# A two-stage 3x3 convolution block on one core: six outer sums moved from adding transfers to VectorE, 13 more constant matmuls, another instruction order

## The chip, the core and the metric

The kernel runs on one core of a Trainium2 chip. The core has a matrix engine (TensorE, "PE" in the profile, with its weight loads "PEld"), VectorE ("DVE"), ScalarE ("ACT"), GpSimd ("POOL"), a queue engine that issues most transfers (SyncE, "SP"), and 16 DMA engines. Each engine works through its own queue in order and waits on semaphores for the others. The metric is device time of one execution in microseconds (us).

## The reference

```python
B, C, HW, E = 2, 512, 64, 1152
def gn(z, gamma, beta):            # group norm, 4 groups of 128 channels
    ...
def conv3(z, w):                   # 3x3, padding 1, as nine shifted einsums
    ...
h = conv3(_silu(gn(x, g1, be1)), w1)
h = h + (_silu(t_emb) @ w_emb).reshape(B, C, 1, 1)
h = conv3(_silu(gn(h, g2, be2)), w2)
return x + h
```

Two images of 512 channels, 64 x 64 points; two group norms with silu, each followed by a 3x3 convolution from 512 to 512 channels; a per-channel embedding is added between them and the input at the end. Inputs are bf16, the kernel computes in f16 with sums in f32.

## The kernel before

**Tiling.** Channels are cut into four tiles of 128 (the partitions): `ct` of the input, `k` of the output. Each image is cut into two halves of 32 rows, so there are eight chunks `c`: 0 and 1 the halves of image 0 in the first convolution, 2 and 3 those of image 1, 4 to 7 the same for the second. A unit is one chunk and one output tile (`unit(c, k)`, L818): 32 units.

**Fewer products.** The convolution over rows is done as a fast algorithm: VectorE forms six combinations ("planes" 0 to 5) of the rows of a chunk (`rows_a`, `rows_b`), VectorE and ScalarE form six combinations of the weights (`prep_w1`, `prep_w2`), TensorE multiplies plane by plane, and the results are added with small factors. Planes 0 to 3 are partly nested a second time over columns (`nest_w1`, `fetch_w2`, `vnest`). In a unit, ScalarE reads the finished sums from PSUM (`evac_o` for planes 4 and 5, `evac_m`, `evac_b`), and VectorE adds them up: S, A, s, d and y (L872 to L1015). The planes 4 and 5, the "outer" ones, must still be added to the first and last eight rows of the unit's result `ys`: the outer sum, 128 x 1040 elements. `CFG['oacc'][c]` says for how many of the four `k` this is done by an adding transfer that GpSimd issues (`dma(yo.ap, oo.ap, ..., sw=True, acc=True)`, named `oa`); for the others it is a `tensor_tensor` on VectorE (named `O`). In chunks 4 to 6 the result then goes to the output by another adding transfer from GpSimd's queue, onto the input that was copied there before (`pre`); in the first convolution it goes to `h_scr`. There are two buffers `ys`, used in turn.

**Opening.** The first image is loaded in eight pieces (`x0` and `x1`: first and second half of a channel tile), with the first weights between. `stats0` makes the group norm's sums: tile 0 by `bn_stats` on VectorE for the first half, by ScalarE (a square with its sum) and TensorE (products with ones) for the second; tiles 1 to 3 by TensorE (products with ones, and Gram products for the squares) for the first half, by ScalarE and TensorE for the second. `gn_chain` joins them with a few tiny f32 matmuls, VectorE and GpSimd instructions. Then `silu` (ScalarE) and `rows_a` and `rows_b` (VectorE) make the planes of chunk 0, and TensorE does planes 4 and 5 of units 0 to 2 first ("o"), since these need only `rows_a`. Before all that, TensorE multiplies constants: 11 matmuls `warm` and `CFG['fill']` matmuls `fill`, 128x128 by 128x512 ones into PSUM bank 5, which nothing reads (L1082 to L1085).

**Between.** `stats1` makes the sums of image 1 on ScalarE during chunk 0 (two passes of 2080 elements over each of eight pieces); `prod(c+1, k)` makes the planes of the next chunk while chunk `c` is multiplied; `prep_w2` makes the second convolution's weights and stores them in `u_scr`; `outer_kinds` and `outer_weights` make operands for chunk 7, whose planes 4 and 5 are nested too. The embedding's product is copied from PSUM by VectorE (L1105).

**Order.** Every operation is an `Op` of a plan with an engine and its dependencies. They are emitted in the order that the string `ORDER` gives (two characters for each operation, base 64), so the string fixes the order in every engine's queue. Matmuls of the units follow a chain that fixes their order among each other. All of it goes through a few helper lines, so the profile shows L348 for VectorE's tensor_tensor, L352 for its scalings, L371 for ScalarE, L386 for transfers and L401 for matmuls.

Of the kernel before, what the change touches and what calls it, by code (L numbers as in the profile page):

```python
# [115 lines left out]
def _idx(off, dims):  # L116
# [49 lines left out]


ORDER = (
    "0E09000B0A2T0C0G0F0D0c010H020304050607080b0I160a130R0Z140X0g0S0Y150d0f0e0T0h1817190i0j0U0k1A0l1B0K1C2M1D0m0n1u0L"
    "0o2J0V0W1E0v0M1N1X3C1F0O1G1Y0p1Z0y0J1r0r1a3K1b1_0q1H201Q0N1c2c221d0s211e1I0t1f23241g4g0_1h3E251J0u2U261i271j0w28"  # L170
    "1K291k3F0x100Q0z120-2A3D1L1l2B1M1m1O1n2C4L111P1o1R2f1S4T3H1p2D1q1x2F1s3L2E1t1y1v2G1w1T2e2P2H2i2I3G2K1U2Q1-2L0P2N"
    "2W2O1V2X1z2l2Y1W2m3g2V2Z2R2n2b4O2h2d2o2S2p3a2a2q3X4N2r3M2s3N3h2g4M2t3i3O2u3P2v4U2k2w2x3Q2j2y3R2_2z3S3Z3j3d2-3k3u"
    "303T5P323v3U4V313w4Q3J5H4X3x4W3y3I3V3z4P333-4Y3_343l374Z423c3m3543366L3W443Y4a453b465J4S4h4k4738485K5Q493e394q3r"
    "4b3n4r3o4e4B4s5I4c4t4R3f4u4m4v406D4n4A4w414x4f4j6Y4-5R4_4d6M505T3p6Z513q525L6a535U547u556F5V5S5c4l3s5X4i5d7v5e4C"
    "6E5f7w5h5W5i4D4G4o5jB74EB85k4p3A4F5l5M4H5m5n3t5Z4I5Y5o566G8y575r4z6N5s4y5a5tB9583B5u5b5w6P5x595C5N5y6O5A6Q5z5BBB"
    "5-5v6RBN8z5_5g7h6S6I605D616b4J6T5E6H6c6U6d8l8-6e6XBA6W6g5q6h6iBFBCBP6j6kBD5p6l6mA06n626sBO6VBG636t6JBE5O6KA14K6u"
    "A25F6vB46x646y6w6z6-65686_7071BRBH727666B5BJ6777D56f6978DDBQ7PBIBT796A6o7Q6pBS7A7RB6DE737BBU7S6r5G7TBL7CBK7D7UBM"
    "7V7W7x7X747Y7Z7y7aD67E7b6q7z7c7F7d75DG7-7eDF7f7G80D781827gDH7i8384D985Ee86DJ87DL8C7H8DDI7I7j8E7JD27K8F7l888H7k8G"
    "8I8J8K8m7m8L8M8ND39p8O7n8S7L8T897p8U6B7M7_7o8VDN8A8W8Q7q8a8XD4D88n8Y8PDB8Z8o8_8bDA8p909qDMDC7r918q928BAt947s6C95"
    "9697988r998R9ADK9B9G7t7O8c9HEf8s9IDP9J8tEm9L8d9M9N9O8w8f9P9Q9R8e9S8x9W8g8u9XEg8h939Y9C9ZDOEi8i9D9r9aEuEh9F7N9bAu"  # L180
    "DR9cDQ9s9d9tA39UEn8vA49K9u9TA59ECr9e9vA69V9fA89xA9A7AA8jAB9gACAD9wAE9kAFAK9hAGAHAL9y9jAMEkEoAvAN9iEjAPEpAQAxElCs"
    "ARAS9-ATAUAVAWAa9lEvAbDS9zAX9mAcAyAYAdAw8kAeAzEO9_AfAIA_AgAiA-AhAJBVAjB09nBWEwAZCtBXB3AkBYB2BaBbAoBcAlBdAOBeBfCv"
    "AnBgBhBlCuAmBmBnBjBoApBiBtBZBuBpCwAqBkBvEyBq9oBwEbGJB1ByBzCQEqB-B_CREcC0GBC1CxExC2CTEdC3BxC6CUCzC7C8C4C9EsCCCAEr"
    "CDC5CyEtAsCEE-CVC-CFFxEzDTBrGLDUC_GDGKE_CGDVCSBsEPCWD1DWGCD0DYDZDaDbCBDcDdDgDeDfGFEQDjCXCHDkDlCYG8DmDrGNDhCZCIDs"
    "HhGECaGRG9DtCKCbERGMDuCLCJCcESDwFyDxDyCdGADzD-CeETD_E0E1CME4HUE5E6DoE7DnEAGHDiCNCfEBDXEUArGPE2ECGGDvEVEDGSHjEWF0"
    "GTCgGOE3F1GIChE8EXF2DqFzF3CiDpGQF5CjEaF6F7GVF8F9EEE9FAHpFBFCFEFGHVHlFHFIFJEFHxFOEYHiFPCkF_GUFQEGFLFREZEIFTEJFUEH"
    "FVG0FWFFFXFYF4GWFZFaEKFDFdFeHrFfFgHkFjG1FKELClGXFkFbF-HqFSFlGYJ6FMFcFmHtFhCOG2GZCPCmHnGaCnHmGbG3GcHzFNHyI3FnG5Ge"
    "GfJ7GgHsG7GhGiG4GnGjGmGkGlFiHWGpJ8GqHoGrGsHuGxFoEMGyHvGuKNGoGzFpGtCpG-HYI4FrHwFsH0G6H1H2ENH3H4CoHZH5H6H7FqHAHaHB"
    "FtHCHDH-HGG_HXFuHHGdGwKPHII5KOHbHEHJCqHcI6IBH9GvHKICHdNMH8IDHgJ9HfIENLIGHFIHIIIJIKI7ILIMHLINIRIQISH_ITHPIUHMIZIP"
    "I0IOIaHOHNI9IbIWI1IVIcIFI8I2HeIeJAIfHQIgIhFvIiIjIkIlIXHRIoInIpJCIqIAIdIrIuIYImJDIvIsJBIwJEItKQIxJGJSJLJFJTJUJHIy"  # L190
    "JJJVKRJXJYJZIzJaJbJcI-FwJdMvJeLeJiKTJjLfJkJlJIJqKSJ0JrKUOzI_JsJ1JKJtLgJfMxO-J2KVJvJwJgJxJhJyMwKXJzJ-JWJ_KWK0JnK3"
    "K4JuJMK5K6JmKbK9K1KYKAK2KaK7KBLhKCKZKjKcJNKkJoKDKlJ3LiKmJpJOKoKpKqK8KrKsKnKtKuLkKvKxKzMyJPK-HSK_L0KEL5LlL6LjLmL7"
    "KFKIOiL8OjKwJQLAKHNHNGLBLoLCKGLDLELnQBLFKyLGJRLHHTLKLLOkLpNJLMLNLQLrLROxL1L2KJLSMzQALTLsL-L4L_L9M_LIM0M-LJM1N0Pv"
    "LUM3L3PwM4LOM5KdM6N1M7M8LPM9J5MAJ4MEMFKeMGMHLVMMLqNKMCMNMDLWMOLZKKLXMPN2MBKLMRLYMSKfMTMUM2MVN3MWMJMXPxLtMIMYLaMb"
    "KMMcMdMeMhN6MiMQMLMjMZN4MkMaMKNNMfN7NOMlOyKgOlNPMgN8NQOHN5NSNTMmNUNVOmNWLbNXNYNZOIKhNbMnNcMqOKOnNdMoOoR5RMMpNFNe"
    "KiLdNgNhMrQ8NiNjNkNlNmOpLcNnNRNrNsMsNtOqNuNvLuNaNwQ9NxNyOrMuN-OLLvN_O0O1OsO2O3O4LwO5O_NfOMOJLxNoP0ONOwP1NzNpP2Nq"
    "O6P4OtP5P6PyP7O7OOP8P9PAOPPBLyPDO8PzPELzPFRKO9PGN9OAR7PIR6P-PJOCPKPLNAOBPMPNP3POOvPPMtPTPCPUPVPWP_PXPQPYPZRLODPa"
    "PcPHPdPePfQ0PgOEPhPiSZPRPjQ1QCPSOFPkQDOuTlPbQESHNINBQFQ3R8QHPlSIQIOGQJQKQLQMQ2QNQOQQPmNCQRPqPnQSQ5PoQTQ4PpQVSXQW"
# [1192 lines left out]
```

## Time and profile before

| | us |
|---|---|
| three runs | 460.74, 462.39, 459.73 |
| median | 460.74 |
| the profiled execution | 462.31 |
| its span, first to last instruction | 460.5 |
| TensorE busy | 448.6 |
| VectorE busy | 436.9 |
| ScalarE busy | 402.8 |
| GpSimd busy | 57.8 |
| mean granted TensorE clock | 0.992 |

The page gives each engine's busy time over the span; the 40 slices show it over time, in tenths; the table of stages gives it in us for any stretch, with the granted clock, the share of the DMA engines and GB/s at the end of the line. The groups of instructions have a mean duration, in which neighbours overlap, so what one more instruction costs is read from start to start. The list of waits says who waited for whom. An operation's place in the order string is matched to the trace by counting each engine's instructions. Twenty-six adding transfers `ar<-ar` are in the profile, 22 of 260 KB and 4 of 130 KB (the outer sums of the first two units of chunk 4 are done in two pieces).

### The profile page before, as it was taken

The numbers are of one execution on the slowest core, as the hardware profiler recorded it, in microseconds if no ns is written. First come the engines' busy times: TensorE is split into PE (matmuls) and PEld (weight loads), VectorE is DVE, ScalarE is ACT, GpSimd is POOL, SyncE is SP. The second block draws the span as 40 slices with busy tenths as digits, with TensorE's granted clock in tenths as the row PEclk, the third lists the DMA queues.
The fourth block names the chain that finished last, engine by engine and source line by source line (L and its number), as shares of the span: only waits on it lengthen the run. The fifth ranks groups of instructions, "written<-read, shape, count | busy, mean of one in ns | idle before, by whom it ended". The sixth has DMA issues, their size and how long they took to land. (4 is left out here: it accounts for less than half of the span.)

```text
span 460.5 us, 8098 instructions
## 1 busy us (share of the span) xinstructions
PE 448.6 (97%) x2891; PEld 282.0 (61%) x2891; DVE 436.9 (95%) x811; ACT 402.8 (87%) x611; POOL 57.8 (13%) x82
## 2 busy tenths in 40 slices
PE   9799999999999999999999999999999999999995
PEld 5644334455555566566665666776666667787882
DVE  2999997999999999999999999999899999999995
ACT  5799999999999999999999999868989869757662
POOL 2110010111111101111000001212221223121210
PEclk9979999999999999999999999999999999999999
DMA  8962371487557467577877947788896999776764
GB/s 322 398 243 71 124 238 47 141 255 214 165 175 212 122 190 224 149 243 220 257 231 231 357 177 218 190 225 231 176 238 164 268 227 252 164 186 121 165 109 93
DMA packets 43176, 92.49 MB, mean 201 GB/s; under 512 B 6400, under 2 KB 18048, under 8 KB 43136
## 3 DMA queue, kind: packets, MB, share of 16 engines
q1 hardware_dynamic: 32208, 77.60, 49.9%
q0 software_dynamic: 10640, 14.38, 19.7%
q8 instruction: 22, 0.36, 0.3%
q14 instruction: 18, 0.15, 0.1%
q10 hardware_dynamic: 288, 0.01, 0.0%
HBM read 62.25 MB, written 31.32 MB: 203 GB/s over the span
## 5 line engine op out<-in xcount | busy, mean ns | idle before, releaser
L401 PE MATMUL psum<-ar 128*128 128x256 f16 (+2 forms) x2771 | 429.6, 317 | 2.7 <-ACT ar L371 1.9
L348 DVE TENSOR_TENSOR ar<-ar 128x1024 f16<-128x1024 f16 (+7 forms) x630 | 413.0, 717 | 7.6 <-ACT ar L371 4.7
L401 PEld LDWEIGHTS <-ar 128*128 128x128 f16 (+1 forms) x2763 | 268.7, 98 | 159.9 <-issue 9.6
L371 ACT ACTIVATE ar<-ar 128x512 f16<-128x512 f16 (+6 forms) x186 | 186.9, 1041 | 24.3 <-DVE ar L348 23.3
L371 ACT ACTIVATE ar<-psum 128x512 f16<-128x512 f32 (+3 forms) x250 | 159.1, 681 | 21.2 <-PE psum L401 13.8
L371 ACT ACTIVATE ar<-ar,fs 128x2112 f16<-128x2112 bf16 (+1 forms) x32 | 68.8, 2154 | 3.5 <-DVE fs L494 2.8
L386 POOL DMA_DIRECT2D ar<-ar x26 | 30.8, 1207 | 217.9 <-DVE ar L348 190.7
L386 POOL DMA_DIRECT2D out_dram<-ar x15 | 18.7, 1244 | 58.6 <-DMA ar<-ar 41.8
L371 ACT ACTIVATION_READ_ACCUMULATOR ar<-psum 128x1 f32 x104 | 22.6, 217 | 0.0
L352 DVE TENSOR_SCALAR ar<-ar 128x520 f16<-128x520 f16 (+3 forms) x50 | 19.5, 402 | 0.0
L390 POOL MEMSET ar<- 128x65 f16 (+4 forms) x29 | 5.8, 270 | 93.6 <-DVE ar L348 48.8
L401 PEld LDWEIGHTS <-ones_bf 128*128 128x128 bf16 x75 | 7.7, 108 | 5.9 <-issue 3.3
L401 PE MATMUL psum<-fs,ones_neg 128*128 128x1 f32 (+3 forms) x36 | 5.4, 263 | 3.0 <-ACT ar L371 2.9
L401 PEld LDWEIGHTS psum<-fs,ones_neg 128*128 128x128 f32 x36 | 5.2, 214 | 4.3 <-ACT ar L371 3.7
L401 PE MATMUL psum<-ones_bf 128*128 128x512 bf16 x19 | 6.8, 536 | 1.1 <-DVE ones_bf L405 1.1
L371 ACT ACTIVATION_READ_ACCUMULATOR ar<-ar 128x1 f32 x36 | 7.2, 201 | 0.0
L401 PE MATMUL psum<-ar,ones_bf 128*128 128x260 bf16 x56 | 7.1, 275 | 0.0
L1125 DVE BATCH_NORM_STATS2 fs<-ar 128x6 f32<-128x512 bf16 x4 | 2.5, 680 | 3.7 <-DMA ar<-in_x_dram 3.7
L479 POOL TENSOR_TENSOR fs<-fs 128x1 f32<-128x1 f32 x4 | 3.0, 744 | 19.2 <-DVE fs L477 18.6
L1105 DVE COPY ar<-psum 2x512 f32<-2x512 f32 x1 | 0.7, 679 | 2.6 <-PE psum L401 2.6
L439 ACT ACTIVATE s_sb<-tparm 128x18 bf16<-128x18 bf16 x1 | 0.2, 218 | 2.9 <-DMA tparm<-in_t_emb_dram 2.9
L438 DVE CAST fs<-gparm 128x16 f32<-128x16 bf16 x1 | 0.2, 174 | 2.7 <-DMA gparm<-in_params_dram 2.7
(54 smaller groups left out, 26.3 us busy)
## 6 DMA issues: line engine op xcount, KB each, us to landing
ar<-in_w_dram SPq DMA_DIRECT2D x36, 384.0 KB, 5.0
ar<-in_x_dram SPq DMA_DIRECT2D x16, 552.5 KB, 4.8
h_scr<-ar SPq DMA_DIRECT2D x16, 520.0 KB, 5.1
ar<-h_scr SPq DMA_DIRECT2D x16, 520.0 KB, 4.7
out_dram<-in_x_dram SPq DMA_DIRECT2D x30, 260.0 KB, 5.9
out_dram<-ar POOLq DMA_DIRECT2D x15, 520.0 KB, 8.2
ar<-in_x_dram SPq DMA_DIRECT2D x13, 520.0 KB, 4.7
u_scr<-ar SPq DMA_DIRECT2D x16, 384.0 KB, 3.9
```

Source lines behind the costliest of these rows:

```text
L348: pl.op("DVE", 0.075 + 0.000521 * out.n, lambda: nc.vector.tensor_tensor(out=out.ap, in0=a.ap, in1=b.ap, op=op), regs(a, b), regs(out), name)
L352: pl.op("DVE", cost or 0.075 + 0.00026 * out.n, lambda: nc.vector.tensor_scalar(out=out.ap, in0=a.ap, scalar1=s, scalar2=None, op0=ALU.mul ...
L371: lambda: nc.scalar.activation(out=out.ap, in_=a.ap, func=func, scale=sc, **kw), regs(*rr), regs(*ww), name)
L386: lambda: eng.dma_start(out=out, in_=in_, **kw), regs(*r), regs(*w), name, lat=3.2 if sw else None, after=after, sw=sw, seq=seq)
L390: pl.op("POOL" if eng == "gpsimd" else "DVE", 0.08 + 0.0005 * out.n, lambda: e.memset(out.ap, v), (), regs(out), name)
L401: nc.tensor.matmul(out.ap, lhsT=lhsT.ap, rhs=rhs.ap, start=st, stop=sp, skip_group_check=True)
L438: nc.vector.tensor_copy(out=fs[:, GB:GB + 4 * CT], in_=gparm[:])
L439: nc.scalar.activation(out=s_sb[:], in_=tparm[:], func=ACT.Silu)
L479: pl.op("POOL", 0.85, lambda: nc.gpsimd.tensor_tensor(out=F(rs, n).ap, in0=N.ap, in1=F(NEGH, n).ap, op=ALU.pow), regs(N), regs(F(rs, n)), ...
L1105: pl.op("DVE", 0.6, lambda: nc.vector.tensor_copy(out=est.ap, in_=pe.ap), regs(pe), regs(est), nm)
L1125: pl.op("DVE", 0.61, lambda: nc.vector.bn_stats(out=q.ap, in_=e.ap), regs(e), regs(q), nm)
```

## The change

The change has three parts: `oacc` falls from 4 to 2 for chunks 4, 5 and 6, so the outer sums of units k = 2 and k = 3 of these chunks are made by VectorE; `fill` rises from 8 to 21; and the order string is another one. No function is changed.

```diff
-    'oacc': (4, 4, 4, 0, 4, 4, 4, 0),
+    'oacc': (4, 4, 4, 0, 2, 2, 2, 0),
     'ym': (1, 1),
     'km': 1,
     'warm': 11,
-    'fill': 8,
+    'fill': 21,
...
 ORDER = (
-    "0E09000B0A2T0C0G0F0D0c010H020304050607080b0I160a130R0Z140X0g0S0Y150d0f0e0T0h1817190i0j0U0k1A0l1B0K1C2M1D0m0n1u0L"
...
+    "0R0M000j0N0O2h0Q0S0T0p010m0U0203040l05060n0708090k0A0V0o0q0r0s0e1G0t0u0f1H1J0v0w0x0y0g1I0z0B0C0D0E0F1L0-160X0_0h"
...
```

The 13 new operations are numbered right after the old `fill`, so every later number rises by 13; with that the two strings can be laid beside each other. Of VectorE's 790 operations of before some 380 are not in their old order any more, of ScalarE's 468 some 210, of GpSimd's 19, of the transfers 104 of 213, of TensorE's 11, all of these in the opening and in the group norms.

- Transfers in the opening, before: x1 of tile 0, x1 of tile 1, x0 of tile 1, x0 of tile 0, w1, x0 and x1 of tiles 2 and 3. After: x1 and x0 of tile 0, x0 and x1 of tile 1, w1, x0 and x1 of tile 2, x0 of tile 3, a piece of raw weights for unit 1, x1 of tile 3.
- TensorE in the opening, after: `warm`, 10 `fill`, sums of tile 0, first sums of tile 1, group norm 0, rest of tile 1, 5 `fill`, group norm 1, 6 `fill`, sums of tile 2, first sums of tile 3, group norm 2, one `o` group, last sums of tile 3, five more `o` groups, group norm 3, the other `o` groups. Before: `warm`, 8 `fill`, sums of tile 0 and 1, group norms 0 and 1, sums of tile 2, first sums of tile 3, group norm 2, last sums of tile 3, one `o` group, group norm 3, the other `o` groups.
- ScalarE in the opening, after: squares and sums of tile 0, the same of tile 1, silu 0, squares and sums of tile 2, silu 1, squares and sums of tile 3, silu 2. Before: squares of tiles 0 and 1, sums of both, silu 0, silu 1, squares and sums of tile 2, squares and sums of tile 3, a pass over image 1, silu 2.
- VectorE: the six outer sums stand behind the y of their unit; four of them (units 2 and 3 of chunks 4 and 5) ahead of the last planes of chunk 7, the two of chunk 6 behind these.

More of the change, by code (lines that the diff above doesn't have):

```diff
@@ L174 @@
[L174 to L198, printed above, removed]
@@ new lines @@
+    "1K0Z1M190G0H0I0J0Y2Z25100K0L3S1k1N121O1l111a1P131n1Q2p1m0W1C3X2C1R1D1p1S1o2D0a1T220b1q1d3P141r1s2F2E1t1E1u1U150i"
+    "0P1v2G174g1w2H1V1x181W1A1F2W1B1X2I3U0c1Y1y1Z2J2K3R1b2L1-2M1c1z2g1e2N2O1_2P1f1g2028211h293T232Q242R262S3Q272T1j2U"
+    "2c2V2r2s2X2A2Y2j2d2a2B2k2b2l2v3t2i2m2y0d4b3Y2z2e2-1i4t2_2u4h302f312t322q3u3Z333v3V3b342n3n3k354c3c364Y2w373d384d"
+    "3a392x3A3e2o3B3f3C453i3D3w3E3j463x3q3F475X3m3G483g493l3h5c4i4A3p4B4Z4C4j4F4k4G4x3K4H4a4l3y4m4I3H3z4o4J3J5U3o4K3I"
+    "5d4L3L4u4M3s513M4N524n4D533r5Z544p3-4r553_5e6Y4E564-4O574w4z585B4s5V5f5C5g5D4q405h5E5W3W5i5F415G5k425Y5H5j6Q6l5I"
@@ new lines @@
+    "5l5p7u5m4v5q6m5r6n6Z6T43855s4P5u4Q4T5v4e3N864S5w6a4R5x6R5a4U5y5z4f6c4V6S5-6b6d5_4487625J6eBK634y59645A50BL655K8y"
+    "5b6V5o675L685M694_5O6A5N996B5P5n6CBM5t6f6D3O6g6E9A6o6h6p6U5Q6q6r6j5R6t6u666kBS6vBO6w6F6xBT6W6i6yBa6z609B6-4W736G"
+    "AD74616XAEBN754XBQ766H78BP797A6I7BBb777CBR7DAF7EBU7F7J6KBW6J7KBHDIBcBI7L6LBe7M6s6MDQ7cBV7N6_7d706N7eBJ7O7f7R7gBY"
+    "7PBd7hBX7QDS7iBZ7j7H7k88Bg7G7lBf895S7S7m7n8ADK7o717p728B7q7r8D7s8E7t7I7v8FDR8G8HDM8I8J7T8K8PDU8Q7U7X7w8R7WDF5T8S"
+    "7y8U8V7x8W8X7z8Y8Z7V8aDG8bA08L8f7-7Y8M8g8C8h80Er7Z8z7_8iDJDY8O8j6O818kDH8c828l8d8-Bh8mDT839C8o909D8n848T9E916P9F"
@@ new lines @@
+    "8N929H8e9I9J9K8_9LA19M9N8pB49O9T949U939VDLDV8tDW9W9Q8q9Y9Z95Et9a9b9P9cDO9d8r9eDN9f8s9jA2DZ9G9k7a8u9X9lA49m9h8v9g"
+    "A39nDPB5989oA59p979qD29rA6AG967b9SAHA8AI9REsA78wAJ9s9iALDaAMA9ANAODXAP9tAQARASDc9xAXB6EzAUAY9uATAZDbEv9vB8AaF59w"
+    "ABAcAd8xAeAfB9AgAhAiB7AjAnAAAKAoBA9yEuApAbAqE_Dd9zD3ACArAWAsAVBCAtBBAkAuDeAlBiBDAwDfBjAmAvBkD4BGEbAxBlBFBnBoE-Bp"
+    "A_AyBqBrBsEwAzBtBuF1ByA-BzBEB-GOBxB_B0C49-BwBvC5BmD6B1C6F7ExC1C7C0D5F6F0C9EyCd9_EoCACBEpCCCDC3CECFEqCGCJD7CKGQCL"
+    "CMF2C8CPD8CICeF3CQF8D9F4CRCHCgF9CNCSChC2GWB3DgCiDAB2DhGSDDDiGPEcG8DjCfDEDlCjDCDmDnFBDoDpGeDBDqCTDrDsDtCODwDxEdDy"
@@ new lines @@
+    "GLCkFADzClGMGXE2FCCUDuE3GNCmCVE4EfCXE5CnCYCWE7CoEeE8GRE9EAEgGYEBECGgEDCpGUEED-EHCZDkEIEJEKD_ENDvCqGTCaGZEOEhE6Gf"
+    "E1EPEGGiEQEFE0I0EjFDELGVEiERFEGaG9FFCrEMFGHuEkFIHhFJFKGcFLGAFMCsESFNFOFPEmCbFTFUFVFWEWETFbJJFRGbFcEVGBHvFSFdGdCt"
+    "EUHwGCFeFXFHEXFgFhFYFiFjFQFkElI2FlEYFmGhGDFnFqFfFrCuFsEnFtFwCvFuFZCwFxHiGjCxFaFyGEGkFzGGGmFpHyFoGnGFI8F-GoI4JLI1"
+    "HxFvGpIGCcGlGrGHGsGtGuCyF_GvJKGwGxHjHzGyH0GJH1H2H3H8G0G3H9H-KaEZI3G1HAHlG2HBHkG-I9H5GzCzHDG4KcHEIAHFHGEaHHHIHmG5"
+    "HJHKHNI5KbHOHPC-HnHQGKHTH4HCI6HUGIG_HVD0GqC_HpIHHWHLI7D1HoHMIOH7IBHqIPHRH_HtIQIIHsJMNYIRITH6IUG6IVHrIWIXHSIYHXIZ"
@@ L219 @@
+    "dceLeMeNeOeReSdLeGeTe6eUeVeWdWePeXeYede7eeefeaegeQeheZeiejelekf5gDf6emeof7f8f9esfAebfBfCecfEgCfDddfFfGdefHf0fIdf"
+    "fJf2fKfLf1fPh6fMezfQfRepfSfTfUe_erfVe-fWfYeqfZenfafbetfcfdfefffifjfXevfkfleufmfNfnewfgfofpfOfufvfwfhfxfyg0fzf-f_"
+    "gEg1g3gFgGfrgHg7gIg4gJfqgKgLgNftgMgOgPfsgQgRg2g6gSgTg5gUgYg8gVgZgagbgcgdgeg9gfgAghgggigWgBgjgkgXglgmgngogrgpgsgq"
+    "gtgug_gwh0gxh3h2h1gyh5gvgzh4g-h7h8h9hChAhDhB"
 )
```

49 lines of the change are left out of this document (25 added, 24 removed).

## The prediction

> **What bounds the kernel now.** First the page's busy times and the 40 slices:
>
> ```profile
> PE 448.6 (97%) x2891; PEld 282.0 (61%) x2891; DVE 436.9 (95%) x811; ACT 402.8 (87%) x611; POOL 57.8 (13%) x82
> ...
> PEclk9979999999999999999999999999999999999999
> ```
>
> Three engines are nearly full, so a shift of one is worth only what the other two can follow. The table of stages, in steps of 10 us, shows where each is full:
>
> ```profile
> 20.00:30.00 10.00, 8.70 (x35) 4.63 (x36) 9.09 (x26) 9.49 (x13) 1.99 (x3) 0.66 0.77 289
> 30.00:40.00 10.00, 10.00 (x47) 4.39 (x46) 9.96 (x17) 9.71 (x10) 0.00 (x0) 1.00 0.31 111
> ...
> 70.00:80.00 10.00, 10.00 (x49) 4.60 (x47) 7.43 (x14) 9.97 (x13) 0.00 (x0) 1.00 0.16 54
> ...
> 320.00:330.00 10.00, 10.00 (x68) 6.45 (x67) 8.08 (x15) 9.83 (x10) 1.81 (x3) 1.00 0.75 154
> ...
> 400.00:410.00 10.00, 10.00 (x79) 7.50 (x78) 9.96 (x15) 4.91 (x7) 2.01 (x2) 1.00 0.79 178
> ```
>
> The columns are PE, weight loads, VectorE (DVE), ScalarE (ACT), POOL, granted clock. VectorE is full from 30 to 440 us but for two holes (70 to 80, 320 to 330). ScalarE is full up to 285 us and has room after. PE is full except in the opening, where 20 to 30 us stands out: fewest matmuls, clock 0.66. PE's timeline and a finer table of stages (us, PE busy, clock) tell why:
>
> ```profile
> 17.20 1.24 PE L401 MATMUL psum<-ar 128*128 128x128 bf16 x17
> 21.30 0.83 PE L401 MATMUL psum<-fs,ones_neg 128*128 128x2 f32 x6 [2.87 <-ACT ar L371]
> ```
> ```profile
> 23.40:25.60 2.20, 2.20 (x9) 0.50 0.80 259
> 25.60:30.20 4.60, 4.60 (x13) 0.52 0.52 212
> 30.20:34.80 4.60, 4.60 (x22) 1.00 0.66 239
> ```
>
> PE waits 2.87 us for ScalarE (the sums of channel tile 2), and 2 us after it has work again the clock is at half until 30.2: 13 matmuls where the next 4.6 us hold 22. Lost: 2.20 x 0.50 + 4.60 x 0.48 = 3.3 us, and 2.9 of waiting.
>
> Then the waits of VectorE. The chain that ended last holds 0.9 us, so it says nothing here.
>
> ```profile
> DVE ar L348 <- ACT ar L371: 4.7, 4, 2.3
> ...
> DVE ar L1105 <- PE psum L401: 2.6, 1, 2.6
> ```
>
> The 4.7 us are four waits: 0.5 at 104.9, 1.7 at 324.8, 0.3 at 437.9 and 2.3 at 451.1 us, this last in the tail. The 2.6 is the copy of the embedding (74.6 us), behind which VectorE's queue stands.
>
> Last I matched each instruction to the order string and took, for every matmul, the time from the end of its last VectorE input to its start. The first unit of a chunk needs all four channel tiles of that chunk, and there it is short: 0.6 us in chunks 1 and 3, below zero in chunk 2 (an earlier matmul of its group began first), 0.05 in chunks 5, 6 and 7, 1.7 in chunk 4. So **VectorE's input for each next chunk is what PE runs on**.
>
> **The change, part by part.**
>
> *Six sums.* Six transfers of 260 KB (k = 2, 3 of chunks 4 to 6) become six tensor_tensor of 128x1040. Start to start in an unbroken run these take 0.612 us (median of 197; the row's mean of 696 ns overlaps with the next one). 6 x 0.612 = 3.7 us on a full engine. What goes is POOL's issue (1.2 us each on an engine busy 13%) and the 5.0 us to landing, for which only the output store waits; VectorE's list of waits has no transfer in this stage, so I take 0. The bounds are 0 and 6 x 0.025 us, the mean that a VectorE instruction loses beside a POOL issue (0.017 elsewhere).
>
> *Thirteen constant matmuls.* In the new order two stand ahead of the first sums, five after those of tile 1 and six right before those of tile 2. The last warm ones of before follow each other every 0.216 us: 13 x 0.216 = 2.8 us, the length of the hole. They cost nothing as long as PE would wait there, 2.8 us if it wouldn't, and save the 3.3 us of half clock if PE is busy throughout.
>
> The Trainium skill ("TensorE: Matmul & The Clock Gate", Part 1) says that the clock halves after an idle window of about 3.4 us, and that the window runs freely, so that the cold stretch varies from run to run. The row disagrees in size: 2.87 us were enough here. What the rule would make of it is rival 3.
>
> *The order of the opening.* The first half of x, tile 0, is loaded second instead of fourth. The first four loads land at 4.5, 5.9, 7.2 and 8.6 us, so VectorE's statistics begin at 5.9 instead of 8.6. ScalarE squares tile 0, reads its sums, does tile 1 and goes on to the first silu; the squares of tile 2 are put ahead of the second silu. Chained by the durations of before: silu 0 at 12.9 instead of 14.78 us (held by the second reading of sums), VectorE's first product at 15.1 instead of 17.5, PE's sums of tile 2 at 20.2 behind 13 busy us without a hole. From there VectorE sets the pace: 18.5 us of work up to the last row product of tile 3 (17.2 before) and 1.5 us of dependent pairs and waits, so 35.1 against 36.2 us. PE, which came to its last group of this phase 2.7 us after that product, now comes with it: 35.3 instead of 38.9. **PE gains 3.5 us by 40 us.** VectorE gains 1.1; ScalarE ends its fourth silu at 32.0 against 32.2 and gains 0.2.
>
> *ScalarE up to 105 us.* It waits for PE at 39.7, 43.1 and 52.4 us (0.3 + 0.65 + 0.65); with PE 3.5 us ahead these go: 1.6. Then it has no gap until 102.2 us (0.5, again for PE). So it gains 0.2 + 1.6 + 0.5 = 2.3 us. VectorE's 2.6 us at the embedding go too, but at 104.9 us it waits for ScalarE behind the same amount of ScalarE work in either order (90.05 us, summed as below): it can't gain more than 2.3 there either. The ends of this term: 1.0 (waits come back elsewhere) and 3.5 (as much as PE).
>
> *The order from 105 us on.* I summed the VectorE work that stands ahead of the last input of each chunk's first unit (median durations, each order): chunk 2 137.6 before and 136.7 after, 3 190.0 and 189.5, 4 240.1 and 241.3, 5 292.4 and 291.7, 6 337.7 and 337.8, **7 383.3 and 386.8**. So up to chunk 6 the order costs at most 1.2 us, and chunk 7 pays nearly the whole price: four of the six sums (2.4) and 1.0 of other work stand ahead of its input. Directly dependent neighbours (0.12 us each) rise from 39 to 44 there: inside the rounding.
> With 2.3 us at 105 and 0.4 of small waits of VectorE (about 0.1 each) gone, it is 2.7 ahead at 320 us. The wait of 1.66 at 324.8: VectorE comes 2.7 earlier and has 1.2 more ahead of it, its input comes with PE, 3.4 earlier; the wait closes. That makes 4.4. Less the work ahead of chunk 7 and of its constant products (3.1 to 3.5, taken 3.3): **1.1 us left at 411 us**.
>
> *The end.* Behind 411 us PE runs through; in before it loses 1.2 us there (0.5 at 415.9, the rest to 422). The two sums that stand after chunk 7's input land in that stage, where ScalarE has room: I give back 0.4 of the 1.2. The tail, 5.2 us from the last matmul, is not touched.
>
> Sum: 1.1 + 0.4 = 1.5 us. The profiled execution took 462.31 us (span 460.5 and 1.8 around it): 460.8. It lies 1.6 above the median of the runs (460.74; 459.73 to 462.39); on the median it makes **459.2 us**.
>
> **Rivals.**
>
> 1. *The opening's gain is kept.* ScalarE follows PE, because the second image's statistics (16 readings of 1.92 us, in its queue from 24 to 102 us) can wait until 105.8. Then VectorE is 3.5 ahead at 105, 3.9 at 320, 5.6 behind the hole; less 3.3 makes 2.3, and all of the 1.2 at the end: 3.5 us, 457.2. For it: these 31 us. Against: at 104.9 us the same amount stands ahead.
>
> 2. *VectorE has no room (slower).* The place is the input of chunk 7. If ScalarE gains nothing in the opening, VectorE is level at 105, and the 1.66 us close only by the 1.2 of work moved ahead: 1.2 - 3.3 = -2.1; ten more dependent neighbours in all, 1.2 us, of which I count 0.4: 2.5 us slower, 463.2. It decides from the point where VectorE gains under 3.3 us before 411. For it: 9.96 to 10.00 of 10 us nearly everywhere. Against: the waits named above are real holes.
>
> 3. *The cold stretch isn't in every run, or the constant matmuls don't prevent it.* The three runs differ by 2.7 us, nearly the 3.3 of the stretch, and the profiled one is the slow end. Then the median has part of this gain already and the order's costs stay: about 460.2 us. The freely running window of the Trainium skill (same page and section) would make it so.
>
> **Chances.** Half a per cent, 2.3 us, is about what a measurement of this kernel can tell from no change. Forecast 0.40 (0.34 within, 0.06 faster); rival 1 0.32 (0.30 faster, 0.02 within); rival 2 0.16 (0.13 slower, 0.03 within); rival 3 0.12 (0.09 within, 0.03 slower). Faster 0.36, same 0.48, slower 0.16. The range takes in most of rival 1 and of rival 2: 456.6 to 463.0.
>
> **What would show it.** In the profile of the changed kernel: the clock 1.00 from 20 to 30 us and no PE wait over 1 us there; the last matmul before the first main unit at about 39 us instead of 42.9; no VectorE wait for PE at the embedding; VectorE's busy time up by 3 to 4 us; the first unit of chunk 2 about 2.5 us earlier, that of chunk 7 only about 1. The forecast is wrong if ScalarE's gaps between 100 and 155 us don't shrink (rival 2), if the 1.66 us wait comes back at another unit, or if chunk 7 starts over 2.5 us earlier (rival 1).

## The result and the profile after

| | us | executions | profiled execution (span) |
|---|---|---|---|
| before | 461.50 (459.63 to 463.93) | 12 | 462.31 (460.5) |
| after | 463.81 (462.32 to 465.77) | 12 | 462.32 (460.6) |

Medians with their ranges. The ratio is 1.0057, 95% interval 1.0036 to 1.0077: the change makes the kernel slower by about 2.3 us. The forecast was 459.2 (456.6 to 463.0); sign and size were both missed. The two profiled executions are of equal length, and that misleads: that of before is one of its longer executions, that of after its shortest.

The same lines as in the prediction, from the page of the changed kernel:

```profile
PE 446.7 (97%) x2904; PEld 281.6 (61%) x2904; DVE 442.1 (96%) x817; ACT 402.4 (87%) x611; POOL 50.6 (11%) x76
...
PEclk9999999999999999999999999999999999999998
```

VectorE has 5.2 us more work (3 to 4 were expected), GpSimd 7.2 less, and the slice with the low clock is gone. The stages that the prediction showed, with the hole (18.4 to 21.3) and the half-clock stretch (25.6 to 30.2) of before; columns PE, weight loads, VectorE, ScalarE, GpSimd, granted clock, DMA share, GB/s:

```profile
20.00:30.00 10.00, 10.00 (x58) 5.67 (x57) 9.69 (x25) 9.89 (x11) 2.46 (x5) 1.00 0.71 267
30.00:40.00 10.00, 9.62 (x44) 4.08 (x42) 9.90 (x17) 9.97 (x15) 0.17 (x1) 1.00 0.05 9
70.00:80.00 10.00, 10.00 (x49) 4.61 (x48) 9.10 (x23) 9.45 (x11) 0.00 (x0) 1.00 0.63 208
320.00:330.00 10.00, 10.00 (x69) 6.52 (x67) 9.01 (x14) 9.63 (x10) 1.35 (x2) 1.00 0.91 226
400.00:410.00 10.00, 9.73 (x77) 7.36 (x76) 10.00 (x17) 5.66 (x7) 2.41 (x2) 1.00 0.72 150
18.40:21.30 2.90, 2.90 (x33) 2.42 (x32) 2.90 (x9) 2.35 (x3) 0.00 (x0) 1.00 1.04 402
25.60:30.20 4.60, 4.60 (x26) 2.45 (x25) 4.46 (x11) 4.57 (x6) 1.06 (x2) 1.00 0.28 110
```

The opening does what was forecast: clock 1.00 in these stages, 58 matmuls from 20 to 30 us instead of 35, 33 of them where the hole was, and 26 instead of 13 in the stretch of half clock. VectorE's two holes shrink; its line behind the second one, of before and then of after:

```profile
324.77 2.59 DVE L348 TENSOR_TENSOR ar<-ar 128x2048 f16<-128x2048 f16 x3 [1.66 <-ACT ar L371]
```
```profile
322.69 2.59 DVE L348 TENSOR_TENSOR ar<-ar 128x2048 f16<-128x2048 f16 x3 [0.92 <-ACT ar L371]
```

What the opening gives is lost again, a part of it in chunk 2 (0.39 us at 152.5 and 0.52 at 168.7, both waits for VectorE) and the most behind 265 us. TensorE's timeline shows where (start, us of the run of matmuls, and in brackets the idle time before it and what ended it; five of its lines):

```profile
268.98 5.89 PE L401 MATMUL psum<-ar 128*128 128x256 f16 x40 [1.85 <-ACT ar L371]
309.76 55.43 PE L401 MATMUL psum<-ar 128*128 128x512 f16 x386 [0.19 <-DMA ar<-in_w_dram]
366.59 43.15 PE L401 MATMUL psum<-ar 128*128 128x256 f16 x319 [1.40 <-ACT ar L371]
411.19 6.38 PE L401 MATMUL psum<-ar 128*128 128x256 f16 x57 [1.46 <-DVE ar L348]
418.32 1.92 PE L401 MATMUL psum<-ar 128*128 128x256 f16 x16 [0.75 <-DVE ar L348]
```

Two waits for ScalarE in units (4,0) and (6,0), one for weights that come late, and two for VectorE at chunk 7's input and its constant products (the matmuls `C_mms` of chunk 7's nested planes 4 and 5). Before has one of the five, the first, at 270.46 with 1.04; its other waits there are of 0.4 us at most.

Matching the matmuls to the order string gives the start of the same work in each profiled execution, in us. "before" is the execution that the prediction worked with, "before again" another execution of the same kernel; the last two columns are experiments below. The last `o` group is the group of channel tile 3, and of the constant products the one of channel tile 3 is taken.

| start of | before | before again | after | constants alone | constants and sums |
|---|---|---|---|---|---|
| last `o` group | 38.86 | 36.41 | 35.04 | 36.01 | 36.11 |
| chunk 1 | 94.94 | 92.49 | 91.49 | 92.09 | 92.19 |
| chunk 4 | 258.68 | 256.26 | 256.39 | 255.87 | 256.25 |
| chunk 5 | 309.91 | 307.52 | 308.08 | 307.14 | 307.48 |
| chunk 6 | 360.23 | 357.86 | 357.87 | 357.48 | 358.29 |
| chunk 7 | 410.10 | 407.75 | 408.81 | 407.35 | 409.36 |
| chunk 7's constant products | 418.53 | 416.18 | 418.99 | 415.78 | 418.40 |
| span | 460.5 | 458.2 | 460.6 | 457.8 | 460.4 |

Against the first column the change is 3.8 us ahead at 39 us, 1.3 at 409, and level at the end. Against the second it is 1.4 ahead, then level at chunk 4, and 2.4 behind at the end.

### The profile page after: what moved, and what is told of

Read it like the earlier page. It is cut to its first block, busy times and chain, and to the rows that moved or that the text cites. A ratio compares the mean times of both kernels' runs of the same rounds, so it can differ in the third digit from the quotient of the medians.

```text
span 460.6 us, 8091 instructions
## 1 busy us (share of the span) xinstructions
PE 446.7 (97%) x2904; PEld 281.6 (61%) x2904; DVE 442.1 (96%) x817; ACT 402.4 (87%) x611; POOL 50.6 (11%) x76
## 5 line engine op out<-in xcount | busy, mean ns | idle before, releaser
L348 DVE TENSOR_TENSOR ar<-ar 128x1040 f16<-128x1040 f16 (+7 forms) x636 | 418.2, 719 | 7.0 <-ACT ar L371 3.0
L371 ACT ACTIVATE ar<-psum 128x512 f16<-128x512 f32 (+4 forms) x250 | 159.5, 682 | 29.5 <-DVE ar L348 12.6
L386 POOL DMA_DIRECT2D ar<-ar x20 | 23.0, 1177 | 159.0 <-DVE ar L348 125.2
L401 PEld LDWEIGHTS <-ones_bf 128*128 128x128 bf16 x88 | 8.7, 102 | 6.8 <-issue 1.9
L401 PE MATMUL psum<-ones_bf 128*128 128x512 bf16 x32 | 8.8, 431 | 1.1 <-DVE ones_bf L405 1.1
L401 PE MATMUL psum<-ar,s_sb 128*2 128x512 bf16 x9 | 2.7, 377 | 0.0
```

The source lines that it names most:

```text
L348: pl.op("DVE", 0.075 + 0.000521 * out.n, lambda: nc.vector.tensor_tensor(out=out.ap, in0=a.ap, in1=b.ap, op=op), regs(a, b), regs(out), name)
L371: lambda: nc.scalar.activation(out=out.ap, in_=a.ap, func=func, scale=sc, **kw), regs(*rr), regs(*ww), name)
L386: lambda: eng.dma_start(out=out, in_=in_, **kw), regs(*r), regs(*w), name, lat=3.2 if sw else None, after=after, sw=sw, seq=seq)
L401: nc.tensor.matmul(out.ap, lhsT=lhsT.ap, rhs=rhs.ap, start=st, stop=sp, skip_group_check=True)
```

## The experiments

The theory behind the forecast was that the opening's gain passes through VectorE and is mostly spent on the sums. The rivals that the result leaves: the base was wrong (the half-clock stretch isn't in every execution); the sums cost more than their place in the queue; the new order costs by itself; the constants cost. All kernels compute the whole reference. Times are medians, with range and number of executions; the ratio is to before on the same chip, with its 95% interval. The shortest execution of before is 459.40 to 459.53 us in each of the five sets of runs, so times of different sets can be laid beside each other. The letters by which the expectations call theories are explained in each of them, and mean different things in the first groups and in the last one.

### The base: before again, and the constants alone

The first is the kernel before without an edit.

> The kernel of before, unchanged, for the spread of its executions. Theory A (VectorE's work ahead of chunk 7 gives the opening's gain back) says nothing of the spread. Theory B (the half-clock stretch at 20 to 30 us is not in every execution of before): its executions fall in two groups about 1.7 us apart, the slower with a mean clock near 0.992 and the faster near 0.997 or above. If the clock is the same in both groups, the spread has another cause.

Measured: 459.90 us (459.44 to 462.62, 12), ratio 0.9982 (0.9958 to 1.0006). Its profile, of an execution with a span of 458.2 us, shows TensorE's same hole, in one line of the timeline:

```profile
21.73 0.83 PE L401 MATMUL psum<-fs,ones_neg 128*128 128x2 f32 x6 [2.87 <-ACT ar L371]
```

and, in the table of stages, no half clock behind it:

```profile
20.00:30.00 10.00, 8.03 (x46) 4.54 (x47) 9.70 (x26) 9.75 (x12) 1.99 (x3) 1.00 0.77 289
```

Clock 1.00 and 46 matmuls, where the profile shown first has 0.66 and 35. All later stages come 2.3 to 2.5 us earlier, with the same waits. In five sets of runs, 129 executions of before, 63 have a mean clock of at most 0.992 (median 462.38 us) and 66 at least 0.993 (median 459.73), and no time lies between 461.11 and 462.04. So by the times the stretch is in about half of the executions; it is worth 2.65 us between the medians and 2.3 between the two profiles, and it isn't part of the kernel's work. The mean clock alone is no sure mark of it: 14 of the fastest executions (459.40 to 459.64) have 0.993, and the mean also takes in the end of the span, where the clock is at half for 0 to 2.7 us in the 20 profiles. Within the groups, 24 of the 66 lie at 460.32 to 461.11 and 12 of the 63 at 463.69 to 464.01; no profile of before shows what these have.

The second adds the 13 constants to before, all ahead of the group norm's matmul behind the hole.

```diff
-    'fill': 8,
+    'fill': 21,
```

> Before with the 13 constant matmuls alone, all put into the hole ahead of the group-norm matmul of tile 2; order and transfers of before. Theory A: the clock is 1.00 from 20 to 30 us, PE is 3 us earlier at 40 us, the VectorE wait at the embedding shrinks, and 1 to 2 us are left at chunk 2 and later, less than the 3 us: 459.5 to 460.5. Theory B: it equals the faster group of before's executions, 460.6, and has no slower group.

Measured: **459.63 us** (459.46 to 460.76, 12), ratio 0.9961 (0.9943 to 0.9979). All 12 have a clock of 0.997 or more, and none is in the longer group. The hole is filled (start of chunk 1: 92.09 instead of 92.49):

```profile
20.00:30.00 10.00, 9.70 (x53) 5.09 (x52) 9.71 (x26) 9.75 (x14) 1.99 (x3) 1.00 0.76 286
```

What follows: the constants do what they were costed for, but a median over executions gets about half of it. Of all kernels of the study only this one and the one with a single sum behind chunk 7's input, below, have an interval that lies under 1.

### The constants in the new order

The changed kernel without the 13 constants:

```diff
-    'fill': 21,
+    'fill': 8,
```

> The changed kernel without the 13 more constant matmuls, same order else. Theory A: the order alone has closed the 2.9 us hole; without the constants PE has two holes of 1.1 and 1.3 us at 12 to 15 us, the clock may or may not drop; if it does, the opening loses up to 3 us and VectorE's pace hides most of it: 0 to 1.0 us slower than the changed kernel. Theory B: without a stretch the clock is 1.00 and the time the same within 0.5 us.

Measured: 463.09 us (462.41 to 463.39, 12), ratio 1.0044 (1.0026 to 1.0063), all 12 at a clock of 0.997 or more. In the new order the longest holes of the opening are 0.90 us (at 13.19) and 0.61 (19.62) without the constants, and the clock holds. So there they prevent nothing: the order has closed the hole itself. Nor do they cost anything that shows: the changed kernel's two sets of executions have medians of 463.81 and 462.94.

### The sums, by their place

Constants alone, with the six sums on VectorE, and nothing else of the new order:

```diff
-    'oacc': (4, 4, 4, 0, 4, 4, 4, 0),
+    'oacc': (4, 4, 4, 0, 2, 2, 2, 0),
```

> Before's order with the 13 constant matmuls in the hole (459.6 us measured) and the six outer sums on VectorE, each at the place where its transfer was issued. Theory A (the sums take VectorE's time ahead of chunk 7): four sums ahead of chunk 7's input and two behind it, 2.4 to 3.7 us slower than with the transfers: 462.0 to 463.3. Theory C (the new order behind the opening costs, not the sums): within 0.7 us of 459.6.

Measured: 462.14 us (461.70 to 464.26, 12), ratio 1.0025 (1.0002 to 1.0047): 2.5 us more than the constants alone. Chunk 7 starts 2.0 us later in the profiled executions, its constant products 2.6, and behind the start of chunk 7 a wait for VectorE is new:

```profile
410.64 4.75 PE L401 MATMUL psum<-ar 128*128 128x256 f16 x42 [0.46 <-DVE ar L348]
```

Then by place: only the sum of unit (6,3), which stands behind chunk 7's input, `'oacc': (4, 4, 4, 0, 4, 4, 3, 0)`:

> Before's order with the 13 constants in the hole (459.6 us measured), and one of the six sums on VectorE: unit 3 of chunk 6, whose place in VectorE's queue is behind the last input of chunk 7. Theory A (only work ahead of chunk 7's input is paid): 459.6, within 0.25 us. If every sum on VectorE costs its duration: 460.2.

Measured: 459.70 us (459.42 to 460.89, 12), ratio 0.9973 (0.9947 to 0.9998): 0.07 more than the constants alone. And the two of units (4,3) and (5,3), which stand ahead of it, `'oacc': (4, 4, 4, 0, 3, 3, 4, 0)`:

> The same with two of the six sums on VectorE: unit 3 of chunks 4 and 5, both ahead of the last input of chunk 7. Theory A: 2 x 0.61 = 1.2 us slower, 460.6 to 461.0. If VectorE has room of its own: 459.6.

Measured: 460.72 us (459.97 to 461.48, 12), ratio 0.9982 (0.9955 to 1.0009). The profiled execution has an opening that is 1.2 us later (the last `o` group at 37.24 instead of 36.01) at a mean clock of 0.994; six of these 12 executions, and five of the 12 with the sum behind, have spans longer by that much at 0.996 or less. The profile shows why: TensorE waits 1.43 us in the middle of the first sums, ahead of the 13 constants, and the clock is at half from 13.97 us on for 3.4 us. Its lines of the timeline and of the table of stages (0.60 us and 1.00 with the constants alone):

```profile
11.98 1.47 PE L401 MATMUL psum<-fs,ones_neg 128*128 128x2 f32 x12 [1.43 <-DVE fs L1130]
```
```profile
10.00:20.00 10.00, 8.57 (x76) 7.18 (x75) 8.93 (x28) 6.18 (x9) 1.80 (x4) 0.83 1.04 404
```

So with the 13 constants in before's order the clock still isn't full in every execution. For the sums, the stages are counted from the last `o` group. From there chunk 7's constant products start after 379.77 us with the constants alone, 379.67 with the sum behind, 380.29 with the two ahead and 382.29 with all six, and the span ends after 421.75, 421.66, 422.27 and 424.27. **A sum behind chunk 7's input costs nothing; two ahead of it cost 0.5 us, six (five of them ahead) 2.5.** The expectation for all six counted four ahead; but in before's order the sum of unit (6,2) stands ahead too: it starts at 408.64 us, and VectorE's last input of chunk 7's first products at 409.88. Two are not 1.2 because VectorE's hole takes up one of them. Its line with the constants alone, then with the two sums (with all six the hole is 0.94):

```profile
322.00 5.89 DVE L348 TENSOR_TENSOR ar<-ar 128x2048 f16<-128x2048 f16 x8 [1.65 <-ACT ar L371]
```
```profile
323.16 5.89 DVE L348 TENSOR_TENSOR ar<-ar 128x2048 f16<-128x2048 f16 x8 [1.05 <-ACT ar L371]
```

With five ahead that makes 3.1 less 0.7, or 2.4; 2.5 were measured at VectorE's last input of chunk 7 too (383.34 instead of 380.83 from the last `o` group). Operation by operation VectorE falls back by 0.58 to 0.60 us at each of the five and gets 0.71 back at the hole; the 0.26 that are left it has lost before the first sum, by 240 us. The prediction's price of a sum is right, but without the hole, which it counted apart as a gain.

The reverse, the changed kernel with all adding transfers back:

```diff
-    'oacc': (4, 4, 4, 0, 2, 2, 2, 0),
+    'oacc': (4, 4, 4, 0, 4, 4, 4, 0),
```

> The changed kernel with its order and its constant matmuls, but the six outer sums as adding transfers again. Theory A: the PE waits of 1.6 and 0.9 us at the start of chunk 7 go, the time falls by 2.0 to 2.5 us against the changed kernel (463.8), to about 461.5, level with before. Theory C (the new order behind the opening costs, not the sums): the time stays within 0.7 us of the changed kernel.

Measured: 474.24 us (471.84 to 475.57, 6), ratio 1.0280 (1.0245 to 1.0316), 10 us slower than with the sums (in the profile 3.4 us at half clock, from 421.7 us, are a part of it). Its list of waits has an entry that before lacks:

```profile
ACT ar L371 <- DMA ar<-ar: 11.6, 4, 3.5
```

ScalarE waits four times, 11.6 us in all, for an adding transfer (`ar<-ar`). In the new order it reads planes 4 and 5 into the outer buffers earlier, while a transfer still reads them; a sum on VectorE frees the buffer sooner. So order and sums belong together, and the price of a transfer isn't only that of its issue.

To see whether transfers could relieve VectorE elsewhere, two outer sums of chunk 3 were made transfers in the kernel with the constants alone, `'oacc': (4, 4, 4, 2, 4, 4, 4, 0)`:

> The other direction: before's order with the 13 constants, and two of the outer sums of chunk 3 (units 0 and 1), which VectorE makes in both kernels, as adding transfers, each issued at the place of the sum. Theory A: VectorE has 1.2 us less ahead of chunks 5 to 7, so up to 1.2 us faster, 458.4 to 459.2. If ScalarE then waits for a transfer before it can write the outer buffer again, as it did for 11.6 us with the changed order and six transfers: 460 or more.

Measured: 463.53 us (462.17 to 465.17, 12), ratio 1.0049 (1.0021 to 1.0077), 3.9 slower than the constants alone; seven of the 12 executions have a clock of 0.995 or less, and the five at 0.999 (462.17 to 462.47) are 2.7 slower. ScalarE's timeline has it waiting for the transfer, and TensorE's, 16 us on, for ScalarE:

```profile
254.29 0.60 ACT L371 ACTIVATE ar<-psum 128x512 f16<-128x512 f32 x1 [2.55 <-DMA ar<-ar]
```
```profile
270.13 2.13 PE L401 MATMUL psum<-ar 128*128 128x256 f16 x17 [3.32 <-ACT ar L371]
```

### The order, by stretches

Three kernels join the two orders at a point; all have 21 constants. The first has the changed order up to the first matmul of chunk 1, then before's, with all transfers:

```diff
+ ORDER: changed order up to unit (1,0); the remaining operations in before's order
+ 'fill': 21, 'oacc': (4, 4, 4, 0, 4, 4, 4, 0)
```

> The changed order only up to the start of chunk 1, with the 13 constants, then before's order with six transfers. PE is 1.5 us earlier at 40 us than in a before without the stretch. Theory A: VectorE's inputs for chunks 2 to 7 decide and ScalarE holds them at 105 us; 0 to 1.2 us are left: 458.4 to 459.6. If the opening's gain is kept whole: 458.0.

Measured: 460.37 us (460.16 to 461.20, 12), ratio 0.9990 (0.9972 to 1.0008). The new opening has its last `o` group at 35.52 (36.01 with the constants alone), but at chunk 1 TensorE waits 0.75 us for VectorE (at 94.89), and from chunk 2 on the profiled execution runs 0.9 to 1.1 us later than that with the constants alone; between the medians it is 0.7, where both theories had it level or faster. The gain of the opening doesn't reach chunk 2 without the order behind it.

The second has the changed order up to the first matmul of chunk 4 and before's from there:

```diff
+ ORDER: changed order up to unit (4,0); the remaining operations in before's order
+ 'fill': 21, 'oacc': (4, 4, 4, 0, 4, 4, 4, 0)
```

> The changed order with the 13 constants up to the start of chunk 4, before's order with six transfers from there. At that point the changed kernel is level with a before that has no half-clock stretch (256.4 us both), so 459.2 to 460.0, if the front costs nothing.

Measured: 462.64 us (461.91 to 463.18, 12), ratio 1.0031 (1.0013 to 1.0050). It is 3.0 slower than the constants alone, where level was expected if the front costs nothing. In the profiles it is 0.8 behind already at chunk 4 (256.64 against 255.87; after itself is 0.5 behind there). At the joint TensorE waits 0.95 us at 260.42, and 1.67 instead of 1.07 at 270.15, both for ScalarE; from there the waits are those of before.

The third is the reverse: constants alone up to chunk 4, the changed order with its sums from there:

```diff
+ ORDER: constants alone up to unit (4,0); the remaining operations in the changed order
+ 'fill': 21, 'oacc': (4, 4, 4, 0, 2, 2, 2, 0)
```

> Before's order with the 13 constants up to the start of chunk 4, the changed order with the sums on VectorE from there. Theory A and C both: the change's cost lies behind chunk 4, so 462.0 to 463.2, as the changed kernel. If the front of the change costs too, it is 459.6 to 461.

Measured: 465.23 us (462.73 to 466.93, 6), ratio 1.0101 (1.0069 to 1.0133). Four of the six executions have a clock of 0.990 to 0.996; the other two took 462.73 and 464.18 us. It has the waits of after behind 265 us, the first of them 2.48 instead of 1.85. What follows: the rear of the new order loses time in whatever front it gets, and its front doesn't help before's rear either. How much each costs, these three can't say, since a joint leaves ScalarE with work that neither order has there.

### Why executions of after differ by up to 2.6 us

The executions of after have spans from 460.5 to 463.1 at clocks of 0.997 to 1.000. The first guess was a load that stands behind others in SyncE's queue: the second half of the weights of unit (5,0), for which TensorE waits at 309.8. It was moved ahead of the loads that stood before it in the order string (rows of chunk 6 from `h_scr`, and weights of unit (5,1)):

```diff
+ ORDER: `st_0`, the second half, ahead of `st_1` and the first `a61`, which stood before it
```

> The changed kernel with one transfer moved: the second half of unit (5,0)'s weights, issued ahead of the first h_scr load of chunk 6 instead of behind it and two more. Theory D (this load, behind loads that wait in SyncE's queue, makes the spread of the changed kernel): the PE wait for it at 309.8 us goes, the executions lie within 0.6 us of each other, at 462.0 to 462.6, and the chunk 7 waits stay. If the spread has another cause: 462.3 to 465.8 as before the move.

Measured: 463.51 us (462.02 to 464.87, 12), ratio 1.0055 (1.0028 to 1.0083), spans 460.2 to 463.1. The wait at 309.8 is gone from the profile and the spread isn't: alone, that is not the cause.

Then the changed kernel itself, for profiles of other executions, and one with 15 constants (the last six left out):

> The changed kernel unchanged, beside its variant with fewer constant matmuls on the same chip. The executions of the changed kernel run from 460.6 to 463.1 us in span, those of the variant with 8 constants from 460.6 to 461.6. Theory A (the 13 constants themselves delay TensorE in some executions, by up to 13 x 0.216 = 2.8 us, when the sums they stand before are ready early): spread again 460.5 to 463, and a profile of a late execution is behind already at the last o group (after 35.04 us). Theory B (the spread arises behind 250 us, at ScalarE's or transfers' waits): the same opening within 0.2 us and a difference that appears at one stage.

> The changed kernel unchanged, one look, for a profile of another execution. The two theories as in the first of these runs: if its span is over 461.5 us, A shows it late by the difference at the last o group, B has it level there and late from one stage behind 250 us.

> As the one before: one more execution of the changed kernel, with its profile.

```diff
-    'fill': 21,
+    'fill': 15,
```

> The changed kernel with 15 constants: the last six, right before the sums of tile 2, are left out. Theory A: the spread shrinks to about half, median between 463.1 and 463.8. Theory B: the same as the changed kernel on the same chip.

Measured: after 462.94 us (462.43 to 464.87, 8), ratio 1.0054 (1.0034 to 1.0075), and 462.27 and 463.60 in the two single executions; with 15 constants 462.71 (462.00 to 463.71, 10), ratio 1.0042 (1.0017 to 1.0067). With 15 constants the spans go from 460.2 to 461.9 and the median is 0.2 lower than after's beside it: the last six constants hardly cost time, and what they do to the spread ten executions can't say. The three profiles have spans of 463.1, 460.5 and 461.8 and part at two different places. That of 461.8 is late by 0.8 us already at the last `o` group (35.85). Its first run of constants takes longer; first the line of the first execution of after, then of this one:

```profile
1.06 6.14 PE L401 MATMUL psum<-ones_bf 128*128 128x512 bf16 x21 [1.06 <-DVE ones_bf L405]
```
```profile
1.06 7.49 PE L401 MATMUL psum<-ones_bf 128*128 128x512 bf16 x21 [1.06 <-DVE ones_bf L405]
```

Of these 21 matmuls 7 start 0.43 us apart and the others 0.22 in the first, 13 in the second: the execution begins at half pace, for a time that varies (the granted clock of the profiles says 1.00 there). That of 463.1 is late by only 0.16 us there and 0.1 at chunk 5; it then loses TensorE's time to the weights of unit (5,0):

```profile
310.80 51.58 PE L401 MATMUL psum<-ar 128*128 128x512 f16 x364 [1.09 <-DMA ar<-in_w_dram]
```

and 1.3 us more at unit (6,0). There the adding transfer of unit (5,1) lands at 356.6 instead of 354.2. ScalarE, about to read into the same buffer, waits for it, and VectorE for ScalarE. ScalarE's and VectorE's line of the first execution of after, then of this one:

```profile
354.27 0.60 ACT L371 ACTIVATE ar<-psum 128x512 f16<-128x512 f32 x1 [1.06 <-DMA ar<-ar]
355.43 4.32 DVE L348 TENSOR_TENSOR ar<-ar 128x1040 f16<-128x1040 f16 x6 [0.56 <-ACT ar L371]
```
```profile
356.63 0.60 ACT L371 ACTIVATE ar<-psum 128x512 f16<-128x512 f32 x1 [2.40 <-DMA ar<-ar]
357.79 4.33 DVE L348 TENSOR_TENSOR ar<-ar 128x1040 f16<-128x1040 f16 x6 [1.89 <-ACT ar L371]
```

So each of the two theories holds for a part. To test the second part, the sum of unit (5,1) was put on VectorE as well, alone and together with the earlier weight load:

```diff
-    'oacc': (4, 4, 4, 0, 2, 2, 2, 0),
+    'oacc': (4, 4, 4, 0, 2, 1, 2, 0),
```

> The changed kernel with the outer sum of unit (5,1) also on VectorE, so that ScalarE's next reading into that outer buffer (unit (5,3), 354 us) has no adding transfer to wait for. In the profiles of the changed kernel this transfer lands between 353.9 and 356.6 us, ScalarE and then VectorE wait for it (VectorE 0.6 in the 460.6 us execution, 1.9 in the 463.1 us one). Theory T (the spread is made by late transfers): ScalarE's wait for a transfer at 354 us gone, spans 460.3 to 462.0 instead of 460.5 to 463.1, median 462.3 to 462.8. Rival V (VectorE simply has no room): 0.6 us more in every execution, spread as before, median about 463.6.

> The same with the second half of the weights of unit (5,0) loaded ahead of the two transfers that it stood behind, so that both late transfers found in the profiles are taken out. Theory T: all spans within 460.2 to 461.2, median 462.0 to 462.4. Rival V: as in the run before, 463.5 with the same spread.

Measured: 462.64 us (462.26 to 463.76, 10), ratio 1.0036 (1.0010 to 1.0062), spans 460.5 to 462.0; and 462.59 (462.17 to 463.28, 10), ratio 1.0019 (0.9999 to 1.0038), spans 460.4 to 461.5. With the second transfer out the range shrinks from 2.6 us to 1.5, with both out to 1.1, while VectorE has one more sum. The 1.1 that is left fits the start at half pace: the profile at 461.5 has 14 matmuls at half pace at the start and its last `o` group at 35.95. So the spread is made of three things: two late transfers and the slow start. The least sure of them is the weights' load, since the step from 1.5 to 1.1 rests on ten executions of each kernel. The time was expected to fall to 462.0 to 462.4 with both out and stayed at 462.6; that the sum that was added costs a part of what the transfers gave is likely and wasn't measured apart.

## Why the prediction was wrong, point by point

Three steps failed: "the wait closes. That makes 4.4", where 2.5 us were measured; the end, which lost 1.3 us instead of gaining 0.4; and "on the median it makes 459.2", which credits every execution with a gain that half of them can't have. On the profile the forecast was 460.8 and 462.3 came, level with before.

- **The opening: right.** The last `o` group was forecast at 35.3 and came at 35.04; clock 1.00, no TensorE wait over 1 us, no VectorE wait at the embedding.
- **The half clock, 3.3 us: right as a mechanism, wrong as a base.** It was there in the profile that the sum was made against, and by the times in 63 of 129 executions. Those without it are 2.65 us shorter. Rival 3 named this and got 0.12; its first half, that the stretch isn't in every run, was true, its price for it (460.2 in all) left out what follows.
- **ScalarE and VectorE gain 2.3 us by 105: right.** ScalarE's four waits for TensorE are gone, and its reading behind the last of them starts at 102.50 instead of 104.79. With the 0.9 and 0.5 us of work that the order takes from ahead of chunks 2 and 3 it makes 3.2 and 2.8; VectorE's last input came 3.2 us earlier for chunk 2 (152.48 against 155.68) and 2.5 for chunk 3 (205.93 against 208.41).
- **The hole at 324.8 closes, "that makes 4.4": this step failed.** VectorE's wait there went from 1.66 to 0.92 us, not to nothing. VectorE came to it 1.3 us earlier, about as reckoned (2.7 less 1.2), but its input only 2.1 earlier instead of 3.4. A new wait of 0.56 came at 355.4, behind the adding transfer. VectorE's last input for chunk 6 came 2.5 us earlier than before (361.22 against 363.72), instead of some 4.4. The prediction took that TensorE, 3.4 us ahead, would bring VectorE's input; but TensorE had lost 1.6 of its 3.45 by chunk 5: 0.9 of it in chunk 2, where it waited for VectorE, 0.25 in the last unit of chunk 3, and 0.8 in unit (4,0), where it waited for ScalarE, less 0.35 that came back by chunk 5.
- **The price ahead of chunk 7, 3.3 us: about right.** VectorE's input went from 2.5 ahead at chunk 6 to 0.4 behind at chunk 7 (411.14 against 410.72): 2.9. But a part of the hole's closing and a part of this price are the same thing, as the experiment with two sums shows: 0.6 of the 1.65 went to a sum.
- **The end gives back 0.4: wrong.** The new waits at 411.2 and 418.3 are 1.46 + 0.75 us long where before lost 1.2 in that stage, and the lead of 1.3 at chunk 7 is gone at 422 us. One of the two sums of this stage, that of unit (6,2) at 415.34, stands ahead of the last input of the constant products (418.19 to 418.90).
- **"I take 0" for the adding transfers: wrong in the new order.** With them ScalarE waits 11.6 us for its buffers in it, and one of the 20 that are left still costs up to 1.9 us of VectorE.

With the measured terms the forecast's own sum comes out: 2.5 instead of 4.4 ahead, less 2.9, is 0.4 behind at chunk 7's input, and the profiled executions are level. That is rival 2 in its place (the input of chunk 7) and its condition (under 3.3 us gained before 411), by another cause than the one it named. The median is then worse than level, since before's has the half clock in only half of its executions: from 459.73 (before without the stretch) to 463.26, the median of all 22 executions of after, 3.5 us are lost. The sums, measured apart in before's order, account for 2.5 of it; the rest is the order's waits for ScalarE and the late transfers, less what the opening keeps. This last division is by difference and wasn't measured term by term: why unit (4,0) waits 1.85 us for ScalarE instead of 1.04, and unit (6,0) 1.40, has been seen in every kernel with the new rear but not been taken away.

The Trainium skill ("TensorE: Matmul & The Clock Gate", Part 1) says that the window by which the clock changes runs freely, so that the same kernel has 6, 11 or 14 slow matmuls at its start, and that about 3.4 us of idling halve the clock. The first part agrees with the runs, with 6 to 14 in 20 profiles; for the second, the clock was halved about 2 us behind holes of 2.87 us (in one of two profiles of before) and of 1.43 us (with two sums ahead).

## What to carry to other kernels

Before a change is costed against one profile, look for what differs between executions of the kernel before: the times, with the mean granted clock beside them, and a second profile show which executions carry a stretch of half clock, and a gain that removes it is worth only the share that has it. An instruction added to a full engine costs its whole duration only if it stands ahead of the input that the next stage waits for, and less where a hole ahead of that input takes it up, so count the work ahead of that input, and move the addition behind it where possible. And a transfer that nobody seems to wait for still holds its source buffer: a new order that lets an engine reach that buffer earlier turns it into a wait, whose length differs between executions.

## What the runs showed of the hardware

- After a hole of 2.87 us in TensorE's work the granted clock was halved for 6.8 us in one profile (0.50 and 0.52 from 23.4 to 30.2) and stayed at 1.00 in another of the same kernel; it was halved for 3.4 us behind a hole of 1.43 us in the profile with two sums ahead. With no hole longer than 0.90 us behind the first matmul of the opening (the new order with 8 constants) the mean clock was 0.997 or more in all 12 executions.
- The first matmuls run 0.43 us apart instead of 0.22, 6 to 14 of them depending on the execution. A longer run of constants ahead of the first real sums makes that visible in the time: with 21 in a row the last `o` group came at 34.9 to 35.2 us with 7 to 10 slow, at 35.52 with 12, 35.85 with 13 and 35.95 with 14; with 19 in a row and 12 slow, in the same order, at 35.12.
- The same adding transfer of 260 KB, issued beside an output store of 520 KB, took 7.8 us to land in three executions and 9.1 in a fourth, where the median in the profile of before is 5.0.
